# Hash attention and a mixture of adapters on one core: a bank begun by a copy, block turns and loads moved, products of the second last pair moved

## The chip, the cores and the metric

The kernel runs on one core of a Trainium2 chip. TensorE (PE) multiplies, VectorE (DVE), ScalarE (ACT) and GpSimd (POOL) work element by element, SyncE (SP) issues transfers that 16 DMA engines carry out. The metric is the device time of one execution in microseconds; lower is better. The median over several runs counts.

## What is computed

There are 4 batches of 8 heads, 768 positions and 64 features. Each position of q and k gets a bucket from the signs of six projections; a query sees only keys of its own bucket. Rows whose mask is empty fall back to a mean over all keys, which is why the kernel adds a very small uniform term.

```python
q_bits = (einsum('bhsd,dk->bhsk', q, proj) > 0)      # k the same
mask = q_bucket[:, :, :, None] == k_bucket[:, :, None, :]
scores = where(mask, q @ k.T / sqrt(D), -1e9)
attn = exp(scores - max); attn = attn / (sum(attn) + 1e-9)
x = (attn @ v) as (B*S, H*D)
logits = x @ w_gate                                   # two best of eight experts
delta = sum over the two experts e of w_e * ((x @ A[e]) @ B[e])
out = x + delta
```

## The kernel before, in words

The 32 heads are worked off as 16 pairs (p = 0 to 15, two heads h of one batch each, four pairs to a batch), and each pair in six slots (s = 0 to 5). The order of every engine's queue is written out by hand: `slot` (L698) first emits the scores of the slot, then the list that `work` (L710) has put together for it. All queues run strictly in order, so an instruction that waits holds up all that stand behind it on its engine.

In each slot TensorE makes scores for 1536 columns (`score`, four matmuls of L283) in one of two groups of PSUM banks, and ScalarE exponentiates them into P (L286). Per slot there is room for other work on TensorE: the products of P and v (`pvk`, L303, six per block of keys and per head), the hash of a later pair (`hash`, L193), transposes of q (`trq`, L241), the logits of the adapters (`lgz`, L407) and the products that give delta (`delta`, L506 and L527).

The sum for a head is gathered in one PSUM bank (pool ps_v, one buffer). `uni` (L288) begins that bank: a matmul with a matrix of 2^-56 against the column sum of v, repeated six times, writes 390 columns. `pvk` then adds to it, and `norm` (L321 and L323) divides by the gathered sum on VectorE and frees the bank. Head 1 of pair p-1 is begun in slot 0 of pair p and ended in slot 1; head 0 of pair p is begun in slot 3 or 4 and ended in slot 5.

Other work runs ahead: `loadqk` (L152) loads q of pair p+4 in slot 2 and k of pair p+4 in slot 3 (slot 4 in pairs that have logits), `loadv` (L160) loads v of pair p+2 in slot 2. `turn32` (L180, VectorE) turns 32x32 blocks of q and k into R, four turns per pair, in slots 0 to 3 (`turns`): the last half of k of pair p+2, both halves of q of pair p+3 and the first half of k of pair p+3. `hash` (slot 2) reads R of pair p+2, `sign` (L205) compares, `signs_out` and `signs_in` (L212, L220) carry the signs through DRAM into the operands of the scores (aug). `natcast` (L232) casts q and k on GpSimd, `turnk` (L253) transposes k by DMA, `shift` (L261) moves half of it on GpSimd. `vcast` (L168 to L173) casts v on GpSimd and then forms its column sum in three additions. `to_bf` (L333) and `turn` (L339) prepare x for the logits.

The adapters of batch b are done while batch b+1 is attended to: `plan` (L870) gives each pair which three rows I of logits it makes, in which slot, and which deltas (a dictionary from slot to row). Odd pairs from 5 on have logits in slot 3 (`route1`, `gates`, `gsum`: L416 to L455; the weights' exponential L428 stands on ScalarE ahead of the scores' exponential of slot 4), and from 7 on one delta in slot 0; even pairs from 6 on have two deltas in slots 3 and 4. Logits, hashes, transposes and deltas all use one bank (pool ps_m, one buffer). The last two pairs have an order of their own.

Of the kernel before, what the change touches and what calls it, by code (L numbers as in the profile page):

```python
# [12 lines left out]
F32 = mybir.dt.float32  # L13
# [6 lines left out]
class Emitter:  # L20
# [142 lines left out]
    def vcast(self, p):  # L163
        if p >= self.N:
            return
        nc, T, D = self.nc, self.T, self.D
        vn, vb = self.vn[p], self.vb[p % 3]
        nc.gpsimd.tensor_copy(out=vb[:, :, 0:T, 0:D], in_=vn)  # L168
        s3 = self.smallp.tile([self.P, 2, 3, D], F32, tag="vs3", name=f"vs3_{p}")
        nc.gpsimd.tensor_add(out=s3, in0=vn[:, :, 0:3, :], in1=vn[:, :, 3:6, :])  # L170
        s1 = self.smallp.tile([self.P, 2, D], F32, tag="vs1", name=f"vs1_{p}")
        nc.gpsimd.tensor_add(out=s1, in0=s3[:, :, 0, :], in1=s3[:, :, 1, :])
        nc.gpsimd.tensor_add(out=vb[:, :, T, 0:D], in0=s1, in1=s3[:, :, 2, :])  # L173
# [111 lines left out]
            at += w  # L285
        nc.scalar.activation(out=self.P_[p][:, s * W:end], in_=ps, func=ACT.Exp, scale=128.0)  # L286

    def uni(self, p, h):  # L288
        T, D = self.T, self.D
        pv = self.pv[p, h] = self.vt([self.P, T, D + 1], F32, f"pv{p}_{h}")  # L290
        self.nc.tensor.matmul(out=pv, lhsT=self.eps,  # L291
                              rhs=self.vb[p % 3][:, h, T:T + 1, :].to_broadcast([self.P, T, D + 1]),
                              start=True, stop=False, skip_group_check=True)

    def pvk(self, p, h, kts):
        if p < 0:
# [352 lines left out]
    def first(self, s):  # L649
        if s == 0:  # L650
            self.hash1(1, self.h1)
            self.turn32(1, 0, 0)
            self.turn32(1, 1, 0)
            self.sign1(self.h1, (0, 1))
            self.natcast(1, 0)
            self.natcast(1, 1)
            self.loadv(1)
            self.loadqk(3, 0)
        if s == 1:
            self.hash(1, (0,))  # L660
# [4 lines left out]
            self.vcast(0)  # L665
        if s == 2:
            self.trq(1, 0)
            self.qcopy(1)
            self.shift(1, 0)
        if s == 3:  # L670
            self.trq(1, 1)
            self.qcopy(1, 1)
            self.turn32(1, 0, 1)
            self.turn32(1, 1, 1)
            self.shift(1, 1)
            self.signs_in(1, (0,))
            self.loadqk(4, 0)
            self.natcast(2, 0)
            self.natcast(2, 1)
            self.turn32(2, 0, 0)  # L680
            self.turn32(2, 0, 1)
        if s == 4:
            self.hash(1, (1,))
            self.sign(1, (1,))
            self.signs_out(1, (1,))
            self.loadqk(4, 1)
            self.turn32(2, 1, 0)
            self.signs_in(1, (1,))
            self.vcast(1)
        if s == 5:  # L690
            self.trq(2)
            self.qcopy(2)
            self.turn32(2, 1, 1)
            self.shift(2, 0)
# [15 lines left out]
    def work(self, p):  # L710
        N = self.N
        W = [[] for _ in range(6)]
        add = lambda s, *f: W[s].append(f)
        b, L, Ls, D = self.plan(p)
        n1, n2, n3, n4 = (p + i for i in range(1, 5))
        last = p == N - 1
        new = p == N - 2

        if last:
            pv = {0: [(p - 1, 1, (2, 3))], 1: [(p - 1, 1, (4, 5))]}  # L720
        elif new:
            pv = {0: [(p - 1, 1, (0, 1, 2))], 1: [(p - 1, 1, (3,))], 2: [(p - 1, 1, (4, 5))]}
        elif p:
            d = int(p == 1)
            pv = {d: [(p - 1, 1, (0, 1, 2))], d + 1: [(p - 1, 1, (3, 4, 5))]}
        else:
            pv = {}
        if p == 0:
            pv.update({3: [(p, 0, (0, 1, 2))], 5: [(p, 0, (3, 4, 5))]})
        elif new:  # L730
            pv.update({3: [(p, 0, (0, 1, 2))], 4: [(p, 0, (3, 4, 5))], 5: [(p, 1, (0, 1))]})
        elif p == 1 or L:
            pv.update({4: [(p, 0, (0, 1, 2, 3))], 5: [(p, 0, (4, 5))]})
        elif not last:
            pv.update({3: [(p, 0, (0, 1))], 4: [(p, 0, (2, 3))], 5: [(p, 0, (4, 5))]})

        def values(s):
            for g, h, kts in pv.get(s, ()):
                if kts[0] == 0 and g == p:
                    add(s, "uni", g, h)  # L740
                add(s, "pvk", g, h, kts)
                if kts[-1] == 5:
                    add(s, "norm", g, h)

        if p == 0:
            for s in range(6):
                add(s, "first", s)
                values(s)
        elif p == 1:
            self.second(add, values)  # L750
        else:

            if not last:
                add(0, "uni", p - 1, 1)
            values(0)
            if 0 in D and not last:
                add(0, "delta", *D[0])
            add(0, "turns", p, 0)
            add(0, "shift", n1, 1)
            add(0, "signs_in", n1)  # L760
            add(0, "natcast", n2, 1)

            values(1)
            if last:
                add(1, "to_bf", p - 1)
                add(1, "turn", p - 1)
            add(1, "turns", p, 1)

            values(2)
            add(2, "loadqk", n4, 0)  # L770
            add(2, "loadv", n2)
            add(2, "hash", n2)
            add(2, "turns", p, 2)
            add(2, "shift", n2, 0)
            if last:
                add(2, "lasts", 2)
            else:
                add(2, "to_bf", p - 1)

            add(3, "sign", n2)  # L780
            add(3, "signs_out", n2)
# [12 lines left out]
            if p < 5:  # L794
                add(4, "trq", n2, 1)
                add(4, "qcopy", n2, 1)
            if L:
                for f in ("gates", "zt_dma", "gsum"):
                    add(Ls + 1, f, b, L)
                add(4, "loadqk", n4, 1)  # L800
            values(5)
            add(5, "trq", n3)
            add(5, "qcopy", n3)

        if L:
            for i in L:
                add(Ls, "lgz", b, L, i)
            add(Ls, "route1", b, L)
        for s in sorted(D):
            d, i = D[s]  # L810
            if s or last:
                add(s, "delta", d, i)
            if p < N - 2 and i in (2, 3):
                add(s, "store", d, 1, i % 2)
            elif i % 2:
                add(s, "store", d, i // 2)
        if last:
            for s in range(3, 6):
                add(s, "lasts", s)
        for i, at in enumerate(((1, 5), (2, 4), (2, 5), (3, 4), (3, 5), (4, 4))):  # L820
            if at[0] == p:
                add(at[1], "load_moe", i)
        for i, at in enumerate(((4, 5), (5, 4))):
            if at[0] == p:
                add(at[1], "cast_moe", i)
        return W

    def second(self, add, values):
# [27 lines left out]
        add(3, "turns", 1, 3)  # L856
        add(3, "natcast", 4, 0)
        add(3, "vcast", 2)
        values(4)
# [163 lines left out]
```

## Time and profile before

| what | value |
|---|---|
| three runs | 161.24, 162.39, 164.31 us (median 162.39) |
| the profiled execution | 162.86 us, of which the span from first to last instruction is 161.1 us |
| TensorE busy | 148.5 us (92%) |
| ScalarE busy | 143.0 us (89%) |
| GpSimd busy | 111.6 us (69%) |
| VectorE busy | 108.9 us (68%) |
| transfers | 33.04 MB, mean 205 GB/s |

Most rows below name engine, line, what is written and what is read, how often, and the busy time. A row of the timeline starts with the time in us from the span's start; what stands in brackets at its end is the idle time before it and what ended it. A table by stretches gives for each stretch its length, then the busy time of each engine, the granted TensorE clock, the share of the DMA engines and GB/s. Its stretches here run from the first exponential of one pair to that of the next (pair 6 begins at 61.96 us, pair 9 at 87.12, pair 14 at 131.76).

### The profile page before, as it was taken

The numbers are of one execution on the slowest core, as the hardware profiler recorded it, in microseconds if no ns is written. First come the engines' busy times: TensorE is split into PE (matmuls) and PEld (weight loads), VectorE is DVE, ScalarE is ACT, GpSimd is POOL, SyncE is SP. The second block draws the span as 40 slices with busy tenths as digits, with TensorE's granted clock in tenths as the row PEclk, the third lists the DMA queues.
The fourth block names the chain that finished last, engine by engine and source line by source line (L and its number), as shares of the span: only waits on it lengthen the run. The fifth ranks groups of instructions, "written<-read, shape, count | busy, mean of one in ns | idle before, by whom it ended". The sixth has DMA issues, their size and how long they took to land.

```text
span 161.1 us, 5327 instructions
## 1 busy us (share of the span) xinstructions
PE 148.5 (92%) x2169; PEld 101.0 (63%) x2170; DVE 108.9 (68%) x292; ACT 143.0 (89%) x125; POOL 111.6 (69%) x166
## 2 busy tenths in 40 slices
PE   6988999999999999999999979999979999999830
PEld 3335676676767667676766656667756666689510
DVE  5698985746464976778686676686656545665880
ACT  3688899999999999999999969998997999899640
POOL 7783999998969795969397955979399742620060
PEclk9999999999999999999999999999999999999995
DMA  4994469899998895989979996999978750665055
GB/s 149 320 371 131 133 194 192 225 233 215 214 215 195 241 206 146 247 167 373 198 208 233 291 259 164 225 215 361 233 158 197 232 82 16 119 267 180 6 201 192
DMA packets 57595, 33.04 MB, mean 205 GB/s; under 512 B 42978, under 2 KB 55266, under 8 KB 57570
## 3 DMA queue, kind: packets, MB, share of 16 engines
q1 hardware_dynamic: 57296, 32.43, 79.8%
q8 instruction: 17, 0.28, 0.7%
q10 hardware_dynamic: 274, 0.27, 0.5%
q14 instruction: 8, 0.07, 0.1%
HBM read 20.16 MB, written 7.03 MB: 169 GB/s over the span
## 4 chain that ended last, share of the span: by engine, by line
PE 67%; DVE 11%; DMA 10%; POOL 5%; issue 2%; ACT 1%; DVEq 0%; SPq 0%; POOLq 0%
PE s L283 28%; PE pv L303 16%; DMA nat<-in_k_dram 6%; PE hs L193 6%; DMA aug<-nb 3%; PE tr L241 3%; PE pv L291 3%; PE dl L506 2%; DVE R L180 2%; PE lz L407 2%; PE warm L647 2%; POOL nb L232 1%; DVE aug L571 1%; DVE x L323 1%; DVE aug L590 1%
## 5 line engine op out<-in xcount | busy, mean ns | idle before, releaser
L286 ACT ACTIVATE P<-s 128x1536 bf16<-128x1536 f32 x96 | 133.2, 1454 | 4.0 <-PE s L283 2.7
L283 PE MATMUL s<-aug 71*128 71x512 bf16 (+2 forms) x432 | 78.5, 308 | 0.9 <-DVE aug L571 0.7
L283 PEld LDWEIGHTS <-aug 71*128 71x128 bf16 x432 | 34.6, 97 | 21.4 <-issue 5.5
L303 PEld LDWEIGHTS <-P 128*128 128x128 bf16 x1080 | 42.1, 98 | 8.2
L303 PE MATMUL pv<-vb,P 128*128 128x65 bf16 x1080 | 44.3, 193 | 0.0
L261 POOL COPY aug<-aug 64x768 bf16<-64x768 bf16 x30 | 24.8, 827 | 17.6 <-DMA aug<-nb 13.8
L180 DVE STREAM_TRANSPOSE R<-nat 128x384 f32<-128x384 f32 x62 | 33.2, 559 | 5.6 <-DMA nat<-in_k_dram 4.6
L232 POOL CAST nb<-nat 128x768 bf16<-128x768 f32 x30 | 24.6, 823 | 1.0
L333 POOL CAST xb<-x 128x768 bf16<-128x768 f32 x15 | 12.3, 822 | 11.7 <-DVE x L323 4.8
L527 DVE SCALAR_TENSOR_TENSOR acc<-dl,rt,x 128x512 f32<-128x512 f32 x18 | 13.5, 748 | 7.9 <-PE dl L506 7.9
L323 DVE TENSOR_TENSOR x<-pv,ri 128x384 f32<-128x384 f32 x30 | 16.7, 558 | 1.0
L170 POOL TENSOR_TENSOR vs<-vn 128x384 f32<-128x384 f32 x16 | 15.9, 994 | 0.0
L321 DVE RECIPROCAL ri<-pv 128x6 f32<-128x6 f32 x30 | 5.8, 193 | 14.2 <-PE pv L303 14.2
L247 DVE TENSOR_SCALAR aug<-tr 128x768 bf16<-128x768 bf16 x20 | 11.0, 550 | 5.7 <-PE tr L241 2.3
L193 PE MATMUL hs<-R,hst 128*32 128x192 f32 x240 | 14.0, 332 | 0.0
L168 POOL CAST vb<-vn 128x768 bf16<-128x768 f32 x16 | 13.2, 826 | 0.3 <-DMA vn<-in_v_dram 0.3
L241 PE MATMUL tr<-ident_bf,nb 128*128 128x128 bf16 x120 | 10.0, 219 | 0.9 <-DVE ss L453 0.9
L193 PEld LDWEIGHTS hs<-R,hst 128*32 128x32 f32 x240 | 6.7, 109 | 6.3 <-DVE ri L321 3.8
L291 PE MATMUL pv<-vb,eps 128*128 128x390 bf16 x30 | 10.1, 336 | 0.6 <-DVE gw L436 0.3
L525 POOL TENSOR_TENSOR acc<-acc,x 128x512 f32<-128x512 f32 x2 | 2.5, 1266 | 9.2 <-ACT acc L524 9.1
L241 PEld LDWEIGHTS <-nb 128*128 128x128 bf16 x120 | 7.3, 97 | 1.9 <-POOL vb L173 1.0
L173 POOL TENSOR_TENSOR vb<-vs,vs 128x128 bf16<-128x128 f32 x16 | 7.3, 457 | 1.3
(111 smaller groups left out, 112.1 us busy)
## 6 DMA issues: line engine op xcount, KB each, us to landing
vn<-in_v_dram SPq DMA_DIRECT2D x16, 384.0 KB, 7.1
nat<-in_q_dram SPq DMA_DIRECT2D x15, 384.0 KB
nat<-in_k_dram SPq DMA_DIRECT2D x15, 384.0 KB, 3.5
out_dram<-acc SPq DMA_DIRECT2D x7, 512.0 KB, 3.9
out_dram<-acc SPq DMA_DIRECT2D x9, 256.0 KB, 5.6
dr<-sg SPq DMA_DIRECT2D x14, 48.0 KB, 2.9
aug<-dr SPq DMA_DIRECT2D x14, 48.0 KB
nat<-in_q_dram SPq DMA_DIRECT2D x2, 192.0 KB
```

Source lines behind the costliest of these rows:

```text
L170: nc.gpsimd.tensor_add(out=s3, in0=vn[:, :, 0:3, :], in1=vn[:, :, 3:6, :])
L180: self.nc.vector.transpose(out=self.R[p][:, i, h, :], in_=self.nat[p][:, i, h, :])
L193: nc.tensor.matmul(out=hs[32 * j:32 * j + 32], lhsT=self.hst[:, hf].rearrange("p b i -> p (b i)"), rhs=rhs, start=(hf == 0), stop=(hf == 1 ...
L232: self.nc.gpsimd.tensor_copy(out=self.nb[p][:, i].rearrange("p t h d -> p h t d"), in_=self.nat[p][:, i].rearrange("p h (t d) -> p h t d", ...
L241: self.nc.tensor.transpose(out=tr[:, t, :], in_=self.nb[p][:, i, t].rearrange("p h d -> p (h d)"), identity=self.ident_bf)
L261: self.nc.gpsimd.tensor_copy(out=a[0:64, :, 2 + i, :], in_=a[64:128, :, i, :])
L283: nc.tensor.matmul(out=ps[:, o:o + w].rearrange("p (t c) -> p t c", c=P), lhsT=aug[0:71, kt, 2 * h + 1, :], rhs=rhs, start=True, stop=True)
L286: nc.scalar.activation(out=self.P_[p][:, s * W:end], in_=ps, func=ACT.Exp, scale=128.0)
L291: self.nc.tensor.matmul(out=pv, lhsT=self.eps, rhs=self.vb[p % 3][:, h, T:T + 1, :].to_broadcast([self.P, T, D + 1]), start=True, stop=Fal ...
L303: self.nc.tensor.matmul(out=pv[:, i, :], lhsT=self.P_[p][:, o:o + P], rhs=vb[:, h, kt, :], start=False, stop=(kt == T - 1), skip_group_che ...
L323: nc.vector.tensor_tensor(out=self.x[b][:, :, c:c + D], in0=pv[:, :, 0:D], in1=ri.unsqueeze(2).to_broadcast([P, T, D]), op=ALU.mult)
L527: nc.vector.scalar_tensor_tensor(out=out, in0=ps, scalar=rt, in1=self.x[b][:, i, :], op0=ALU.mult, op1=ALU.add)
```

## The change

- `uni` for head 1 of pair p-1 now takes a whole bank (512 columns) and, for p from 3 to 13 (`seeded`), first makes one more matmul, of 65 columns, that puts the column sum of v of pair p into columns 390 to 454. The `uni` of head 0 of pair p is left out for these eleven pairs. In its place, right after `norm` of head 1 of pair p-1 in slot 1, VectorE copies the 65 columns six times over columns 0 to 389 (`seed`), and the products of head 0 are added to that.
- `vsum` is split from `vcast`: the sum of v of pair p+1 is formed at the start of pair p (before: the sum followed the cast at the end of the pair). `loadv` loads v of pair p+3 behind the k load (before: of pair p+2 behind the q load); pair 2 loads v of pairs 4 and 5.
- `turns` gives other halves to other slots: odd pairs turn both halves of k of pair p+2 in slot 0 and the first half of q of pair p+3 in slot 2; even pairs turn three halves of pair p+2 in slot 0 and the two halves of q of pair p+3 in slots 2 and 3 (or 4).
- `sign` follows `hash` directly in slot 2, ahead of that slot's turn.
- Pair 14: its logits move from slot 1 to slot 2, its deltas from slots 3, 4, 5 to slots 1 and 4, and one delta goes to pair 15, which has four (slots 0 to 3). `turn` moves from slot 3 to slot 4. Three blocks of products that stood in slots 1 and 2 stand in slot 1.

```diff
     def vcast(self, p):
...
+        self.nc.gpsimd.tensor_copy(out=self.vb[p % 3][:, :, 0:T, 0:D], in_=self.vn[p])
+
+    def vsum(self, p):
...
-        nc.gpsimd.tensor_copy(out=vb[:, :, 0:T, 0:D], in_=vn)
...
-    def uni(self, p, h):
+    def uni(self, p, h, nxt=None):
         T, D = self.T, self.D
-        pv = self.pv[p, h] = self.vt([self.P, T, D + 1], F32, f"pv{p}_{h}")
+        n = T * (D + 1)
+        V = self.V = self.vt([self.P, 512], F32, f"pv{p}_{h}")
+        pv = self.pv[p, h] = V[:, 0:n].rearrange("p (t d) -> p t d", t=T)
+        if nxt is not None and self.seeded(nxt):
+            self.nc.tensor.matmul(out=V[:, n:n + D + 1], lhsT=self.eps, rhs=self.vb[nxt % 3][:, 0, T, :],
+                                  start=True, stop=True)
         self.nc.tensor.matmul(out=pv, lhsT=self.eps,
...
+    def seeded(self, p):
+        return 2 < p < self.N - 2
+
+    def seed(self, p):
...
+        pv = self.pv[p, 0] = self.V[:, 0:n].rearrange("p (t d) -> p t d", t=T)
+        self.nc.vector.tensor_copy(out=pv, in_=self.V[:, n:n + D + 1].unsqueeze(1).to_broadcast([self.P, T, D + 1]))
...
         elif new:
-            pv = {0: [(p - 1, 1, (0, 1, 2))], 1: [(p - 1, 1, (3,))], 2: [(p - 1, 1, (4, 5))]}
+            pv = {0: [(p - 1, 1, (0, 1, 2))], 1: [(p - 1, 1, (5,))]}
...
-                if kts[0] == 0 and g == p:
+                if kts[0] == 0 and g == p and (h or not self.seeded(p)):
                     add(s, "uni", g, h)
                 add(s, "pvk", g, h, kts)
                 if kts[-1] == 5:
                     add(s, "norm", g, h)
+                    if g < p and self.seeded(p):
+                        add(s, "seed", p)
...
+            add(0, "turns", p, 0)
             if not last:
-                add(0, "uni", p - 1, 1)
+                add(0, "uni", p - 1, 1, p)
             values(0)
             if 0 in D and not last:
                 add(0, "delta", *D[0])
-            add(0, "turns", p, 0)
+            add(0, "turns", p, 1)
+            if p > 2:
+                add(0, "vsum", n1)
             add(0, "shift", n1, 1)
             add(0, "signs_in", n1)
+            if p == 2:
+                add(0, "loadv", 4)
             add(0, "natcast", n2, 1)
 
+            if new:
+                add(1, "pvk", p - 1, 1, (3, 4))
+                add(1, "delta", *D[1])
             values(1)
...
-            add(1, "turns", p, 1)
 
             values(2)
             add(2, "loadqk", n4, 0)
-            add(2, "loadv", n2)
             add(2, "hash", n2)
+            add(2, "sign", n2)
             add(2, "turns", p, 2)
             add(2, "shift", n2, 0)
+            if p == 2:
+                add(2, "vsum", n1)
...
-            add(3, "sign", n2)
             add(3, "signs_out", n2)
             if p > 4:
                 add(3, "turnk", n2)
             values(3)
-            add(3, "turns", p, 3)
             if not last and p % 2 == 0:
-                add(3, "turn", p - 1)
+                add(3 + new, "turn", p - 1)
             if not L:
                 add(3, "loadqk", n4, 1)
+                add(3, "loadv", n3)
...
                 add(4, "loadqk", n4, 1)
+                add(4, "loadv", n3)
+            add(4, "turns", p, 4)
...
-            if s or last:
+            if last or s > 1:
                 add(s, "delta", d, i)
+            if s == 3 and not last:
+                add(s, "turns", p, 3)
...
     def turns(self, p, s):
-        c = {1: {0: (0, 2), 1: (1, 3), 3: (4, 5)}, 2: {0: (2, 3), 1: (4,), 2: (5,), 3: (6,)}}.get(
-            p, {0: (3,), 1: (4,), 2: (5,), 3: (6,)})
+        c = {1: {0: (0, 2), 1: (1, 3), 3: (4, 5)}, 2: {1: (2, 3), 2: (4,), 4: (5,)}, 4: {1: (1, 2, 3), 2: (4,), 4: (5,)}}.get(
+            p, {0: (2,), 1: (3,), 2: (4,)} if p % 2 else {1: (1, 2, 3), 2: (4,), 3: (5,)})
...
         if p == N - 2:
-            return b, G1, 1, {3: (b, 0), 4: (b, 1), 5: (b, 2)}
+            return b, G1, 2, {1: (b, 0), 4: (b, 1)}
         if p == N - 1:
-            return b, None, 0, {0: (b, 3), 1: (b, 4), 2: (b, 5)}
+            return b, None, 0, {i - 2: (b, i) for i in range(2, 6)}
```

In `turns` the number n stands for pair p+2 (n under 4) or p+3, tensor q (n mod 4 under 2) or k, and the half n mod 2. The entry under 0 is issued at the start of slot 0, the one under 1 at the end of slot 0's products and delta, and those under 2, 3 and 4 in these slots.

More of the change, by code (lines that the diff above doesn't have):

```diff
@@ L165, in vcast @@
             return
+        T, D = self.T, self.D
+        self.nc.gpsimd.tensor_copy(out=self.vb[p % 3][:, :, 0:T, 0:D], in_=self.vn[p])
+    def vsum(self, p):
+        if p >= self.N:
+            return
         nc, T, D = self.nc, self.T, self.D
         vn, vb = self.vn[p], self.vb[p % 3]
-        nc.gpsimd.tensor_copy(out=vb[:, :, 0:T, 0:D], in_=vn)
         s3 = self.smallp.tile([self.P, 2, 3, D], F32, tag="vs3", name=f"vs3_{p}")
@@ L665, in first @@
             self.vcast(0)
+            self.vsum(0)
         if s == 2:
@@ L689, in first @@
             self.vcast(1)
+            self.vsum(1)
         if s == 5:
@@ L858, in second @@
         add(3, "vcast", 2)
+        add(3, "vsum", 2)
         values(4)
```

2 lines of the change are left out of this document (added).

## The prediction

> **What bounds the kernel now.** I read the busy shares first, then a table by stretches of one pair each, then the waits, then ScalarE's and VectorE's timelines where the table shows a bad pair.
>
> ```profile
> PE 148.5 (92%) x2169; PEld 101.0 (63%) x2170; DVE 108.9 (68%) x292; ACT 143.0 (89%) x125; POOL 111.6 (69%) x166
> ```
>
> TensorE and ScalarE are both near full, so an average can't name the bound. The stretches can.
>
> ```profile
> 45.37:53.46 8.09, 8.09 (x130) 5.66 (x129) 4.75 (x12) 8.09 (x7) 6.70 (x9) 1.00 0.85 177
> 53.46:61.96 8.50, 8.50 (x134) 5.98 (x133) 7.40 (x23) 8.48 (x8) 6.05 (x8) 1.00 1.04 211
> 61.96:70.17 8.21, 8.21 (x125) 5.54 (x124) 5.71 (x13) 8.21 (x8) 6.71 (x9) 1.00 0.94 203
> 70.17:78.91 8.74, 8.74 (x135) 6.10 (x134) 6.75 (x21) 8.55 (x9) 6.71 (x9) 1.00 1.06 281
> 78.91:87.12 8.21, 8.21 (x125) 5.54 (x124) 5.72 (x13) 8.21 (x8) 6.70 (x9) 1.00 0.87 206
> 87.12:97.01 9.89, 9.02 (x141) 6.42 (x140) 6.86 (x22) 8.44 (x8) 6.72 (x10) 1.00 1.11 260
> 97.01:105.03 8.02, 8.02 (x123) 5.36 (x120) 5.43 (x12) 8.02 (x8) 6.41 (x9) 1.00 0.84 203
> 105.03:114.19 9.16, 9.12 (x145) 6.54 (x144) 6.87 (x22) 8.47 (x9) 7.00 (x10) 1.00 1.07 287
> 114.19:123.15 8.96, 8.10 (x118) 5.34 (x115) 5.27 (x12) 8.23 (x7) 7.17 (x10) 1.00 0.89 201
> 123.15:131.76 8.61, 8.38 (x128) 5.77 (x127) 4.99 (x17) 8.44 (x8) 5.94 (x9) 1.00 0.68 170
> 131.76:141.04 9.28, 8.94 (x143) 6.55 (x142) 5.14 (x16) 8.67 (x8) 3.82 (x6) 1.00 0.32 65
> ```
>
> These are pairs 4 to 14: length, then busy PE, PEld, DVE, ACT, POOL. Pair 7 (with logits) takes 8.74 and pair 8 (without) 8.21, and TensorE is busy for all of both. Pairs 9 to 12 have the same work as 7 and 8 in turn and take 9.89, 8.02, 9.16 and 8.96; in 9 and 12 TensorE stands idle for 0.9 us. ScalarE's timeline shows why, and its floor:
>
> ```profile
> 94.22 0.22 ACT L428 ACTIVATE e<-d 128x24 f32<-128x24 f32 x1 [1.33 <-DVE d L418]
> ...
> 111.40 0.22 ACT L428 ACTIVATE e<-d 128x24 f32<-128x24 f32 x1 [0.61 <-DVE d L418]
> 111.53 9.48 ACT L286 ACTIVATE P<-s 128x1536 bf16<-128x1536 f32 x7
> ```
>
> Seven exponentials that ran on end took 9.48 us. One lasts 1.45 (the page's mean, 1454 ns), and they overlap a little, so they start (9.48 - 1.45) / 6 = 1.34 us apart: six, a pair, need 8.03 us. No pair can be shorter. The small exponential of the adapters stands ahead of slot 4's and waited for VectorE (d). VectorE in turn waited:
>
> ```profile
> POOL aug L261 <- DMA aug<-nb: 13.8, 8, 3.4
> ...
> DVE R L180 <- DMA nat<-in_k_dram: 4.6, 3, 1.9
> ```
>
> ```profile
> 93.19 0.58 DVE L180 STREAM_TRANSPOSE R<-nat 128x384 f32<-128x384 f32 x1 [1.91 <-DMA nat<-in_k_dram]
> ...
> 110.36 0.58 DVE L180 STREAM_TRANSPOSE R<-nat 128x384 f32<-128x384 f32 x1 [1.18 <-DMA nat<-in_k_dram]
> ...
> 119.41 0.58 DVE L180 STREAM_TRANSPOSE R<-nat 128x384 f32<-128x384 f32 x1 [1.55 <-DMA nat<-in_k_dram]
> ```
>
> All three waits are the turn of the first half of k of pair p+3, in slot 3 of pairs 9, 11 and 12. The logits' maximum (9, 11) and a delta's end (12) stand behind it. So three things bound these stages: TensorE in pairs 5 to 8 and 13, ScalarE in pair 4 and those like it (8.09 against 8.03), late k loads in 9, 11 and 12.
>
> **The change part by part.**
>
> *Turns.* The turn that waited (n = 6) is gone from slot 3. A first half of k loaded in slot 3 or 4 of pair p is now turned in slot 0 of pair p+2 instead of slot 3 of pair p+1: three slots later, 3 x 1.34 = 4.0 us by the spacing above, twice the longest wait of 1.91. What goes is the excess of pairs 9 to 12 over two undisturbed pairs of each kind: 9.89 + 8.02 + 9.16 + 8.96 = 36.03, less 2 x (8.74 + 8.21) = 33.90: **2.13 us**. What is late next is TensorE itself, which is full in pairs 7 and 8. The turns of q keep some six slots from load to turn. The bound below: the waits return elsewhere, 0 gained; the bound above: all three idle times, 4.64.
>
> *The bank.* For eleven pairs TensorE drops a matmul of 390 columns and gains one of 65.
>
> ```profile
> 69.94 0.34 PE L291 MATMUL pv<-vb,eps 128*128 128x390 bf16 x1
> 70.12 0.71 PE L303 MATMUL pv<-vb,P 128*128 128x65 bf16 x18
> ...
> 75.91 0.90 PE L303 MATMUL pv<-vb,P 128*128 128x65 bf16 x24
> ```
>
> ```profile
> 131.63 0.34 PE L291 MATMUL pv<-vb,eps 128*128 128x390 bf16 x1 [0.23 <-DVE x L323]
> ...
> 136.06 0.33 PE L291 MATMUL pv<-vb,eps 128*128 128x390 bf16 x1 [0.32 <-DVE gw L436]
> ...
> 136.78 0.38 PE L506 MATMUL dl<-Bcat,zT 128*128 128x512 bf16 x1
> 136.99 0.81 PE L283 MATMUL s<-aug 71*128 71x512 bf16 x4
> ...
> 149.25 0.22 PE L349 MATMUL pvJ<-vb,eps 128*128 128x65 bf16 x2
> 149.31 0.52 PE L407 MATMUL lzI<-wa,xT 128*128 128x136 bf16 x6
> ```
>
> From start to start the wide one takes 0.18 (69.94 to 70.12), two of 65 columns take 0.06 (149.25 to 149.31), so one 0.03: 0.15 saved per pair. It counts where TensorE is the bound: pairs 5 to 13, nine times 0.15 = **1.35 us**; pair 8's 8.21 - 0.15 = 8.06 still lies above ScalarE's 8.03. In pairs 3 and 4 ScalarE sets the time, and I take 0 (0.05 each at most).
>
> ```profile
> L180 DVE STREAM_TRANSPOSE R<-nat 128x384 f32<-128x384 f32 x62 | 33.2, 559 | 5.6 <-DMA nat<-in_k_dram 4.6 <-DMA nat<-in_q_dram 0.9
> L323 DVE TENSOR_TENSOR x<-pv,ri 128x384 f32<-128x384 f32 x30 | 16.7, 558 | 1.0
> L170 POOL TENSOR_TENSOR vs<-vn 128x384 f32<-128x384 f32 x16 | 15.9, 994 | 0.0
> ```
>
> ```profile
> 72.52 0.56 DVE L323 TENSOR_TENSOR x<-pv,ri 128x384 f32<-128x384 f32 x1
> ```
>
> VectorE gains eleven copies of 390 numbers from PSUM. No row shows a copy within PSUM; the nearest, L323, also reads PSUM and takes 0.56 for 384. I take 0.56 (0.4 to 0.8): 6.2 us of VectorE in all. In pair 7 the copy follows the division that ends at 73.08 and is over at 73.64; the products that need it start at 75.91, so 2.3 us cover it. In even pairs they stand a slot earlier, which leaves about 1 us. Odd pairs lose one turn of 0.56 (three instead of four) and even pairs gain one: VectorE then holds 6.75 + 0.56 - 0.56 = 6.8 us of about 8.6, and 5.72 + 1.12 = 6.8 of 8.06. Cost 0; with the cover gone, up to 0.56 x 11 = 6.2. The 65-column matmul waits for nothing that the wide matmul behind it doesn't wait for; its sum is formed nearly a pair ahead.
>
> *Sums, loads, signs.* GpSimd's order stays what it was but for one thing: from pair 3 on the sum that stood at a pair's end is that of the next pair. That puts one more set of three additions (0.99 the largest, L170) into pairs 2 and 3, under 3 us, and pairs like 4, where GpSimd works 6.70 of 8.09, take that up. Cost 0 (0 to 1.0, if a transpose of q in pair 2 or 3 waits for its cast). One v load more falls into pair 2; no one waits for v. `sign` ahead of a turn leaves 0.56 earlier, and with it signs and the k transposes, which stand next on SP now that the v load is behind k. That shortens GpSimd's wait of 13.8 us, which today delays nothing that ends last: 0. SP also gets v between k and the signs' read (see the third rival).
>
> *Pairs 14 and 15.* Pair 14 loses one delta product (0.21, from 136.78 to 136.99) and the wait of 0.32 ahead of the bank's start, because its division no longer stands behind the route's steps on VectorE; the wait of 0.23 at 131.63 stays. Pair 15 gains the product, ahead of other work in slot 3. I take 0.32 + 0.21 - 0.21 = **0.3 us**. The bounds: pair 14's whole excess, 9.28 - 8.03 = 1.25, gained, or two products (0.42) lost in pair 15. `turn` of pair 14, one slot later, is wanted only at pair 15's end. Nothing else behind 149.3 changes.
>
> *Sum.* 2.13 + 1.35 + 0.3 = 3.8 us off the profiled execution, whose time is 162.86: 159.1. The median of the runs is 162.39, 0.47 lower, which would give 158.6. Whether that 0.47 is in the late loads, which go, or elsewhere, the page doesn't say; I take the middle, **158.9**.
>
> **The rivals.**
>
> *1. The waits for transfers move, they don't go.* The DMA share is 1.07 to 1.11 in pairs 9 and 11, and the change moves no fewer bytes. If the next consumer (GpSimd's 13.8 us wait, or a cast) now ends last, only the bank and the end gain: 162.4 - 1.35 - 0.3 = 160.7. For it: crowded odd pairs. Against: GpSimd works only 6.41 us of pair 10, more idle time than in pair 8, and that pair is the shortest of all with 8.02.
>
> *2. The bank's start gains nothing*, because the copy or the deltas' common bank hold TensorE as long as the matmul did, or ScalarE becomes the bound in all even pairs: 162.4 - 2.13 - 0.3 = 160.0. Against: TensorE is full to the last in pairs 7 and 8, and the copy has 1 to 2.3 us of cover.
>
> *3. Slower: signs come late.* The v load (384 KB) now stands between k and the signs' read on SP.
>
> ```profile
> 88.85 0.29 SPq L220 DMA_DIRECT2D aug<-dr  x1
> ...
> 90.23 0.90 SPq L160 DMA_DIRECT2D vn<-in_v_dram  x1
> ```
>
> ```profile
> 95.98 0.81 PE L283 MATMUL s<-aug 71*128 71x512 bf16 x4
> ```
>
> ```profile
> dr<-sg SPq DMA_DIRECT2D x14, 48.0 KB, 2.9
> ```
>
> ```profile
> 105.74 4.59 DMA nat<-in_k_dram
> ...
> 114.12 5.26 DMA nat<-in_k_dram
> ```
>
> The read is issued at 88.85 and needed by pair 10's first scores at 95.98: 7.1 us, and 1.15 less when pair 9 is no longer stretched (9.89 to 8.74): 6.0. No view shows when it lands. The nearest rows are the signs' write, of the same size, 2.9 us after issue, and the late k loads, 4.6 to 5.3. The v load adds its 0.9 of issue and, as my estimate, as much again for its bytes: 4.7 to 7.1. So it is close. It decides from a landing 6.0 us after the old issue time on. A wait of 1 us ahead of each of pairs 8, 10, 12 and 14 eats the whole gain; 2 us in each gives 158.9 + 8 = 167, the middle of the two 165. For it: the Trainium skill, DMA: Bandwidth & Descriptors, section Queues, rings and completion order, says that each DMA engine takes descriptors in ring order, so that v's bytes go ahead of the signs; no view of this run shows the order on one ring. Against: the signs are also written earlier, since the v load no longer stands ahead of `signs_out`, and the median of 2.9 holds for more reads than the three worst k loads do.
>
> **How the numbers follow.** The forecast with its parts: 0.66, by itself 157.6 to 160.2 (the turns from 1.7 to 2.6, the bank 0.9 to 1.5, the end 0 to 0.9). Rival 1: 0.15, rival 2: 0.11, rival 3: 0.08. Two per cent of 162.39 is 3.25 us, so under 159.1 counts as faster (2% is about what a measurement of this kernel can tell from no change): somewhat over two thirds of the forecast's range by weight, 0.46. Within two per cent: the rest of the forecast, 0.20, rivals 1 and 2, 0.26, and 0.03 of rival 3: 0.49. Slower by more than 2%, over 165.6: 0.05. The range is 157.3 to 161.6: it takes in rivals 1 and 2 and leaves out rival 3 and the tails.
>
> **What would show it.** VectorE's wait for k loads drops from 4.6 to under 1; no idle time over 0.3 ahead of L428 in pairs 9 and 11; pairs 9 and 11 at 8.6, 6, 8, 10 and 12 at 8.05 to 8.15, pair 7 at 8.6; 19 wide starts of the bank and 11 narrow ones, eleven copies near 0.56 with no PE wait behind them; pair 15's first exponential about 0.5 sooner after pair 14's than 9.28. I am wrong if TensorE shows idle time ahead of a pair's first scores (signs), or GpSimd's casts hold up transposes in slot 5, or pairs 9 to 12 still differ from 7 and 8.

## The result and the profile after

The changed kernel takes 160.49 us (median of 20 runs, 158.90 to 163.19), the kernel before 162.52 us in runs beside them (20, 160.91 to 164.89). The ratio is 0.987, with a 95% interval of 0.984 to 0.990: 2.0 us or 1.3% faster, inside the range that was forecast and about 1.6 us short of its middle. (Medians are over all runs, while a ratio leaves out the runs more than 1.5% above the fastest of their kernel.) The profiled execution has a span of 159.5 us and a time of 161.24, 0.75 above the median, so it holds somewhat more idle time than most.

The page's busy time of each engine:

```profile
PE 147.3 (92%) x2168; PEld 100.6 (63%) x2170; DVE 116.2 (73%) x303; ACT 143.0 (90%) x125; POOL 112.0 (70%) x166
```

VectorE has 7.3 us more than before (116.2 against 108.9), 6.3 of it in the copies; TensorE has 1.2 less. The windows by pair, 6 to 14, with the columns as before (length; PE, PEld, DVE, ACT, POOL; clock, DMA share, GB/s):

```profile
61.80:70.24 8.44, 8.37 (x128) 5.70 (x129) 7.23 (x16) 8.20 (x7) 6.35 (x9) 1.00 1.00 209
70.24:78.66 8.42, 8.42 (x134) 5.96 (x132) 6.60 (x21) 8.38 (x8) 6.76 (x9) 1.00 1.25 283
78.66:88.10 9.44, 8.38 (x126) 5.66 (x124) 7.60 (x16) 8.41 (x7) 6.26 (x8) 1.00 0.88 171
88.10:96.69 8.59, 8.59 (x136) 6.12 (x135) 6.15 (x19) 8.44 (x7) 6.92 (x10) 1.00 1.12 296
96.69:105.23 8.54, 8.14 (x125) 5.55 (x124) 7.28 (x16) 8.23 (x6) 6.19 (x9) 1.00 1.07 205
105.23:113.70 8.47, 8.47 (x134) 6.01 (x133) 6.17 (x20) 8.36 (x7) 7.04 (x10) 1.00 1.07 306
113.70:121.87 8.17, 8.17 (x128) 5.56 (x126) 6.96 (x15) 8.17 (x7) 6.45 (x10) 1.00 0.92 196
121.87:130.25 8.38, 8.18 (x127) 5.63 (x125) 6.02 (x19) 8.34 (x9) 7.55 (x11) 1.00 0.77 203
130.25:138.88 8.63, 8.55 (x141) 6.46 (x141) 4.91 (x15) 8.63 (x9) 1.60 (x2) 1.00 0.14 28
```

Pairs 9 to 12 now take 8.59, 8.54, 8.47 and 8.17, together 2.3 us less than before. But pair 8, undisturbed before (8.21), now takes 9.44: 1.2 of the gain went there, and 0.2 to pair 6 (8.21 before, now 8.44). Two groups of VectorE, then the waits:

```profile
L185 DVE STREAM_TRANSPOSE R<-nat 128x384 f32<-128x384 f32 x62 | 33.1, 559 | 0.5 <-DMA nat<-in_q_dram 0.4
L313 DVE COPY pv<-pv 128x390 f32<-128x390 f32 x11 | 6.3, 572 | 0.4
```

```profile
POOL aug L266 <- DMA aug<-nb: 8.7, 6, 3.2
POOL vs L175 <- DMA vn<-in_v_dram: 2.7, 4, 0.9
PE s L288 <- DMA aug<-dr: 1.2, 2, 0.8
```

The turns wait no more for k (4.6 us before; what is left is 0.4 for q). The eleven copies take 0.57 each, and no row of TensorE waits for one; the matmul of 65 columns takes 0.04 from start to start (78.46 to 78.50), where 0.03 was reckoned. GpSimd's wait for transposes fell from 13.8 to 8.7, and it now waits a little for v (vs). New is the last row: TensorE's scores wait for the signs' read (aug<-dr). The two longest waits of TensorE in the pairs, and the one at the end of pair 2:

```profile
36.06 0.51 PE L246 MATMUL tr<-ident_bf,nb 128*128 128x128 bf16 x6 [0.20 <-POOL nb L237]
...
87.19 0.81 PE L288 MATMUL s<-aug 71*128 71x512 bf16 x4 [0.82 <-DMA aug<-dr]
...
104.32 0.81 PE L288 MATMUL s<-aug 71*128 71x512 bf16 x4 [0.40 <-DMA aug<-dr]
```

The first is the end of pair 2 (8.47 long, 8.14 before), the others are the first scores of pairs 9 and 11, waited for at the end of pairs 8 and 10 (in pair 8 TensorE waited another 0.24 for the transposed zT). So part of what the k loads had cost came back as a wait for signs. Why the signs were late stands in SP's timeline (start, time that the issue takes, line):

```profile
72.26 0.35 SPq L556 DMA_DIRECT2D out_dram<-acc  x1
72.66 1.13 SPq L152 DMA_DIRECT2D nat<-in_q_dram  x1
74.22 1.02 SPq L217 DMA_DIRECT2D dr<-sg  x1
75.34 3.30 SPq L258 DMA_TRANSPOSE aug<-nb  x1
78.74 1.38 SPq L512 DMA_TRANSPOSE zT<-zm  x1
80.17 0.57 SPq L152 DMA_DIRECT2D nat<-in_k_dram  x1
80.80 1.82 SPq L160 DMA_DIRECT2D vn<-in_v_dram  x1
82.79 0.30 SPq L225 DMA_DIRECT2D aug<-dr  x1
```

Here the issue of a transfer occupies SP: the transpose holds it for 3.30 us, the v load for 1.82, and the signs' read leaves only at 82.79, 4.1 us into pair 8. The chain of what ended last then has its flight:

```profile
82.79 4.27 DMA aug<-dr
```

### The profile page after: what moved, and what is told of

Read it like the earlier page. It is cut to its first block, busy times and chain, and to the rows that moved or that the text cites. A ratio compares the mean times of both kernels' runs of the same rounds, so it can differ in the third digit from the quotient of the medians.

```text
span 159.5 us, 5350 instructions
## 1 busy us (share of the span) xinstructions
PE 147.3 (92%) x2168; PEld 100.6 (63%) x2170; DVE 116.2 (73%) x303; ACT 143.0 (90%) x125; POOL 112.0 (70%) x166
## 2 busy tenths in 40 slices
DMA packets 57595, 33.04 MB, mean 207 GB/s; under 512 B 42978, under 2 KB 55266, under 8 KB 57570
## 3 DMA queue, kind: packets, MB, share of 16 engines
HBM read 20.16 MB, written 7.03 MB: 170 GB/s over the span
## 4 chain that ended last, share of the span: by engine, by line
PE 53%; POOL 14%; DVE 12%; DMA 8%; ACT 4%; issue 3%; SPq 2%; POOLq 0%
PE s L288 22%; PE pv L323 12%; DMA aug<-dr 5%; POOL aug L266 4%; POOL nb L237 4%; ACT P L291 3%; PE hs L198 3%; DMA aug<-nb 3%; PE dl L526 2%; DVE R L185 2%; DVE acc L547 2%; PE lz L427 2%; POOL vs L175 2%; PE tr L246 2%; PE warm L667 2%
## 5 line engine op out<-in xcount | busy, mean ns | idle before, releaser
L210 DVE TENSOR_SCALAR sg<-hs,ssc 128x192 bf16<-128x192 f32 (+1 forms) x16 | 6.7, 418 | 2.6 <-PE hs L198 1.7
L177 POOL TENSOR_TENSOR vs<-vs 128x128 f32<-128x128 f32 x16 | 7.3, 455 | 1.3
```

## The experiments

The kernels ran in three groups of four, each beside the kernel before: the first two groups on one chip (kernel before: 163.12 and 163.36 us), the third on another (163.23). Each reading of waits or pairs is that of one profiled execution. Where lengths of pairs are given, they run from first exponential to first exponential in ScalarE's timeline. The theory to begin with: the moved turns and the copy give what was forecast, and late signs take part of it back because v stands ahead of them. The first rival: transfers are so full in pairs 7 to 12 that somebody waits whatever the order.

**The changed kernel again** (no edit).

> The changed kernel once more, beside the variants. Over its 20 runs it was 2.0 us faster than before (162.5 to 160.5). Theory (late signs): the turns' gain is partly given back because the v load stands ahead of the signs' read, so this should again be 1.5 to 2.5 us under before, with an idle PE ahead of the first scores of some pairs (wait for aug<-dr, about 1 us in all). Rival (chance): the wait for aug<-dr of 1.2 us belongs to the one profiled execution and is absent here.

Measured: 160.64 us, ratio 0.987 (0.981 to 0.992). The stall was in pair 7 this time (9.82), pair 8 took 8.10. It was again the signs' read, in the chain:

```profile
71.80 6.67 DMA aug<-dr
```

In these two executions of one kernel the place of the longest stall differs and its kind is the same.

**The signs' read ahead of the v load**, which stands behind it in slot 0 of the next pair.

```diff
-            if p == 2:
-                add(0, "loadv", 4)
+            add(0, "loadv", n2)
...
-                add(3, "loadv", n3)
...
-                add(4, "loadv", n3)
```

> As the changed kernel, but the v load stands behind the signs' read (slot 0 of the next pair) instead of ahead of it. Theory (late signs): no PE wait for aug<-dr, and 1.0 to 1.6 us faster than the changed kernel, so 3.0 to 3.6 under before. Rival (chance, or the transfers are simply full): within 0.4 us of the changed kernel, the wait either stays or moves to GpSimd's sums, which now get v half a pair later.

Measured: 163.75 us, with five of six runs from 162.9 to 164.9 and one of 159.5, too uneven for a ratio, and no gain is shown. Of the profiled execution (163.46 us) two waits and a row of TensorE:

```profile
POOL vs L175 <- DMA vn<-in_v_dram: 11.0, 7, 3.1
...
PE s L288 <- DMA aug<-dr: 0.3, 1, 0.3
```

```profile
122.80 0.51 PE L246 MATMUL tr<-ident_bf,nb 128*128 128x128 bf16 x6 [1.34 <-POOL nb L237]
```

In this execution the signs, now ahead, were nearly in time and v was late. (The Trainium skill, DMA: Bandwidth & Descriptors, section Queues, rings and completion order, has each DMA engine take descriptors in ring order; the wait for signs, down from 1.2 to 0.3 us, agrees, though it follows as well from the read's earlier issue.) In pair 12 GpSimd's sum of v waited 2.85 us and the copy behind it 2.13 for a transpose (aug<-nb); its cast (nb) stood behind both, and TensorE's transposes waited for that. "No one waits for v" in the prediction holds only where v is loaded as early as in the kernel before, whose page has 0.3 us of such waits.

**The change without the copied bank.**

```diff
-        return 2 < p < self.N - 2
+        return False
```

> As the changed kernel, but no bank is begun by VectorE: all 30 banks are begun by the wide matmul. My sum priced the copy at 0.15 us in nine TensorE-bound pairs: 1.35 us slower than the changed kernel, and pairs 7, 9 and 11 at 8.6 instead of 8.45. Rival: the copy gains nothing (the division and the common bank hold TensorE as long), under 0.4 us of difference.

Measured: 162.12 us, ratio 0.990 (0.985 to 0.995), against 0.987 with it: by times the copy can't be told from nothing. By pairs without a stall it can. Without it pairs 5, 9, 11 and 13 take 8.41, 8.67, 8.62 and 8.56; with it, in an execution without stalls (the changed kernel without stores, below), 8.31, 8.52, 8.43 and 8.38: 0.10 to 0.19 less each. (The stores aren't the reason: with them, the version with mended ends below has 8.31, 8.42, 8.47 and 8.40.) In pairs 6 and 8 it is 0.09 and -0.02. My estimate for nine pairs, five odd ones at 0.15 and four even ones at 0.04, is 0.9 us.

**The change with the turns where they were.**

```diff
...
-            add(0, "turns", p, 1)
...
+            add(1, "turns", p, 1)
...
+            add(3, "turns", p, 3)
...
-            add(4, "turns", p, 4)
...
-        c = {..., {0: (2,), 1: (3,), 2: (4,)} if p % 2 else {1: (1, 2, 3), 2: (4,), 3: (5,)})
+        c = {..., {0: (3,), 1: (4,), 2: (5,), 3: (6,)})
```

> As the changed kernel, but the block turns stand where they stood before (k's first half in slot 3 of the pair after its load). My sum priced the move at 2.13 us: 1.5 to 2.5 us slower than the changed kernel, with VectorE waiting for k loads (4.6 us before, 0 after) and gaps ahead of the adapters' exponential. Rival (chance): the k waits were those of one execution or came from the old place of the v load, under 0.5 us of difference.

Measured: 163.56 us, ratio 1.002 (0.997 to 1.006). Without the moved turns nothing is gained, and the wait is back:

```profile
DVE R L185 <- DMA nat<-in_k_dram: 3.9, 4, 1.5
```

From 0.987 to 1.002 is 1.5%, about 2.4 us.

**The moved turns alone, in the kernel before** (the edit of the change, nothing else).

```diff
...
+            add(0, "turns", p, 1)
...
-            add(1, "turns", p, 1)
...
-        c = {..., {0: (3,), 1: (4,), 2: (5,), 3: (6,)})
+        c = {..., {0: (2,), 1: (3,), 2: (4,)} if p % 2 else {1: (1, 2, 3), 2: (4,), 3: (5,)})
```

> The kernel before with the new places of the block turns and nothing else. Theory (my sum): 2.1 us under before, no VectorE wait for k loads, pairs 9 to 12 like pairs 7 and 8. Rival (the turns' gain needs the new place of the v load or the earlier sign): under 1 us.

Measured: 161.62 us, ratio 0.988 (0.981 to 0.996). No turn waits for k any more, but pair 12 took 9.97. GpSimd stood still 4.54 us for a transpose (aug<-nb), which landed 7.66 us after its issue; its casts stood behind that, and TensorE's transposes waited for a cast:

```profile
117.01 0.82 POOL L261 COPY aug<-aug 64x768 bf16<-64x768 bf16 x1 [4.54 <-DMA aug<-nb]
```

```profile
121.31 0.51 PE L241 MATMUL tr<-ident_bf,nb 128*128 128x128 bf16 x6 [1.34 <-POOL nb L232]
```

So the turns by themselves bring 1.2% (0.4 to 1.9), nearly all that was measured, and in a kernel that has v where it always was, a stall of the same size appears elsewhere. The order of v and signs alone does not explain it.

**The v load behind q, two slots earlier.**

```diff
             add(2, "loadqk", n4, 0)
+            add(2, "loadv", n3)
...
-                add(3, "loadv", n3)
...
-                add(4, "loadv", n3)
```

> As the changed kernel, but the v load of pair p+3 stands in slot 2 behind the q load, where a v load stood before the change, so neither ahead of the signs' read nor behind it. Theory (crowded transfers: what stands between a k load and the signs' read makes the signs late, and a v load that lands late holds GpSimd's sums): neither wait, 0.8 to 1.5 us under the changed kernel, about 3 under before. Rival (the transfers are full, whatever is put first, something else is late): within 0.4 us of the changed kernel, with the wait on zT, aug<-nb or nat instead.

Measured: 162.15 us, ratio 0.992 (0.988 to 0.996): no better than the change. Nothing waits for signs or v any more, but GpSimd's aug waits 12.7 us for transposes, and in pair 10 (10.16) TensorE waits behind it:

```profile
POOL aug L266 <- DMA aug<-nb: 12.7, 6, 4.8
```

```profile
103.67 0.51 PE L246 MATMUL tr<-ident_bf,nb 128*128 128x128 bf16 x6 [1.30 <-POOL nb L237]
```

The other pairs are nearly undisturbed (pair 11 takes 8.60). With this my theory that the place of v is the cause fell, and the rival that transfers are full was left: its kind of wait came, though not its time, within 0.4 us of the change.

**The ends mended**: the first copied bank is pair 4's, pair 2's sum goes back to its end, one product goes from pair 15 back to pair 14.

```diff
-        return 2 < p < self.N - 2
+        return 3 < p < self.N - 2
...
-            if p == 2:
-                add(2, "vsum", n1)
...
+            if p == 2:
+                add(3, "vsum", n1)
...
-            return b, G1, 2, {1: (b, 0), 4: (b, 1)}
+            return b, G1, 2, {1: (b, 0), 4: (b, 1), 5: (b, 2)}
...
-            return b, None, 0, {i - 2: (b, i) for i in range(2, 6)}
+            return b, None, 0, {0: (b, 3), 1: (b, 4), 2: (b, 5)}
```

> As the changed kernel, but the first pair with a copied bank is 4, so that the sum for pair 3 stands at the end of pair 2 as before, and the delta that went from pair 14 to pair 15 is back in pair 14's slot 5. Theory: pair 2 ends in 8.1 instead of 8.5 (its last cast no longer stands behind the sum) and pair 15 takes 8.4 instead of 8.9 while pair 14 takes at most 8.9: 0.6 to 0.9 us under the changed kernel. Rival: the loss comes back in pairs 3 and 15's end, within 0.3 us.

Measured: 160.39 us, ratio 0.985 (0.980 to 0.990). By times this is the change's own; by pairs, pair 2 is back from 8.47 to 8.13, and pairs 14 and 15 take 8.95 + 8.38 = 17.33 against 8.63 + 8.94 = 17.57 in the change and 17.66 before. Pair 10 still stalls (9.14); TensorE waits 0.43 us there for zT and 0.33 for signs.

**Both, ends mended and v behind q**; against the ends mended:

```diff
+            add(2, "loadv", n3)
...
-                add(3, "loadv", n3)
...
-                add(4, "loadv", n3)
```

> Both mendings at once: the v load behind q, and the two ends. Theory: 1.5 to 2.3 us under the changed kernel, 3.5 to 4.3 under before (ratio 0.974 to 0.978). Rival (transfers are full): the ends' 0.6 to 0.9 alone.

Measured: 162.04 us, ratio 0.985 (0.980 to 0.991), with runs from 159.6 to 164.9. Pair 9 took 9.72, where TensorE waited 1.03 us for the transposed x (xT). The theory fell here too: another order of the same bytes doesn't end the stalls.

**No stores**: the change and the kernel before, both without the stores that run while pairs are still loaded. The expectations call them those of batches 0 to 2. In fact they are those of batches 0 and 1, so half of the output isn't written (the page has 3.88 MB written to HBM instead of 7.03).

```diff
-            if p < N - 2 and i in (2, 3):
-                add(s, "store", d, 1, i % 2)
+            if p < N - 2:
+                pass
             elif i % 2:
```

> The changed kernel without the stores of batches 0 to 2 of the output (they are left out, so most of the output is never written; all else is computed). Theory (the stalls of 1 to 2 us in pairs 7 to 12 come from transfers that are nearly full there, and the stores are the part of them that nothing waits for): pairs 7 to 12 all lie between 8.1 and 8.7, no wait of a sum, a transpose or a product for a DMA over 0.5 us, and the median is 1.0 to 2.0 us below the changed kernel's 160.5: 158.5 to 159.5. Rival (the late landings are the order of the queue alone: signs behind v): the late signs' read stays, with one pair over 9.3, and the median stays within 0.5 of 160.5.

> The kernel before without the stores of batches 0 to 2 of the output (left out, as in the other run). Theory (transfers full): the waits of the block turns for the loads of k (4.6 us before) fall below 1 us and the kernel comes to 159.5 to 160.8, so that the change is worth only the copied bank's 1.0 and 0 to 0.4 beside it between the two kernels without stores. Rival (the turns are too close to their loads with or without stores): the waits for k stay at 3 us or more and the difference between the two kernels without stores is 2.0 or more.

Measured: 158.76 us for the change (6 runs, 158.2 to 158.9; ratio to the kernel before with its stores 0.974, 0.969 to 0.979) and 160.53 for the other (159.7 to 161.4; 0.986, 0.981 to 0.992). Pairs 8 to 10 of the change, then 9 to 11 of the kernel before, both without stores:

```profile
78.63:86.79 8.16, 8.16 (x127) 5.56 (x126) 6.95 (x15) 8.16 (x7) 6.12 (x9) 1.00 1.00 213
86.79:95.31 8.52, 8.52 (x137) 6.12 (x135) 7.22 (x21) 8.47 (x9) 6.74 (x9) 1.00 1.02 202
95.31:103.40 8.09, 8.09 (x127) 5.50 (x126) 6.86 (x15) 8.09 (x6) 6.39 (x9) 1.00 0.99 208
```

```profile
86.52:95.25 8.73, 8.73 (x135) 6.09 (x134) 6.75 (x21) 8.54 (x8) 7.11 (x10) 1.00 0.85 199
95.25:103.46 8.21, 8.21 (x125) 5.54 (x124) 5.74 (x13) 8.21 (x7) 6.07 (x9) 1.00 1.02 202
103.46:112.20 8.74, 8.74 (x135) 6.10 (x134) 6.83 (x21) 8.55 (x9) 6.70 (x9) 1.00 0.95 209
```

TensorE is busy for the whole of each: no stall is left in either, and the turns of the kernel before no longer wait for k at all. The rival that the turns stand too close to their loads, stores or not, falls for this execution. SP's timeline of the change without stores, for the same stretch as above:

```profile
71.65 0.37 SPq L152 DMA_DIRECT2D nat<-in_q_dram  x1
74.18 0.37 SPq L217 DMA_DIRECT2D dr<-sg  x1
74.64 1.39 SPq L258 DMA_TRANSPOSE aug<-nb  x1
77.17 1.18 SPq L512 DMA_TRANSPOSE zT<-zm  x1
78.41 0.58 SPq L152 DMA_DIRECT2D nat<-in_k_dram  x1
79.03 0.47 SPq L160 DMA_DIRECT2D vn<-in_v_dram  x1
79.68 0.29 SPq L225 DMA_DIRECT2D aug<-dr  x1
```

The same transpose holds SP for 1.39 us instead of 3.30, the v load for 0.47 instead of 1.82, and the signs' read leaves at 79.68, 3.1 us sooner at the same place in the work (pair 8 starts at 78.63 and 78.66). Three things did not come as expected. GpSimd's sums of v still waited 0.8 to 1.15 us in pairs 8, 10 and 11 of the change, over the 0.5 of the theory, though TensorE is busy all the same. The change also had one wait for signs where no store could be the reason, ahead of pair 4 (0.70 us). There the issue of the signs' read held SP for 3.10 us, right behind two loads of adapter weights:

```profile
37.76 1.10 SPq L123 DMA_DIRECT2D w<-in_moe_A_dram  x2
39.31 3.10 SPq L225 DMA_DIRECT2D aug<-dr  x1
```

So it need not be a store that SP stands behind. That the stalls in pairs 6 to 12 go with the stores is shown; whether the stores as such count there, or only the 3.15 MB less to move (29.89 instead of 33.04), no run tells apart. And the difference of the two medians is 1.8 us, between the 1.4 at most of the theory and the rival's 2.0. The two profiled executions, which agree with each other in pairs 5 to 13 but for the change, differ there by 76.1 - 74.6 = 1.5 us; the profiled execution of the kernel before is the fastest of its six, and where the others lost up to 1.8 us more isn't recorded here.

**The copy made twice** (each copy of `seed` issued two times).

```diff
+        for _ in range(2):
             self.nc.vector.tensor_copy(out=pv, ...)
```

> The changed kernel with each of VectorE's eleven copies into a bank made twice (same result, 11 x 0.58 = 6.4 us more of VectorE). Theory (the copy lies in cover): within 0.5 us of the changed kernel. Rival (nothing covers it; TensorE's sums of the first head wait for it): 3 to 6 us slower, and the sums of v with the first head wait for VectorE in each pair.

Measured: 161.92 us, ratio 0.994 (0.989 to 0.999) against 0.987: some 1.1 us more. Neither: most of 6.3 us is covered, not all. Rows of VectorE and of TensorE in pair 7 (a line number above 313 is one higher here):

```profile
73.48 1.18 DVE L314 COPY pv<-pv 128x390 f32<-128x390 f32 x2
74.57 0.41 DVE L210 TENSOR_SCALAR sg<-hs,ssc 128x192 bf16<-128x192 f32 x1
```

```profile
75.03 0.87 PE L428 MATMUL lz<-wa,xT 128*128 128x136 bf16 x12 [0.21 <-DVE sg L210]
```

The first to notice isn't the product that adds to the bank but the logits, which wait until the signs behind the copy have been taken out of PSUM. Slot 3 of the odd pairs grows from 1.46 to 1.78 us, so of the 0.6 that the second copy adds (1.18 for two) only about 0.3 was covered. In even pairs it is covered (pair 8: 8.12).

**The best version: ends mended, batch 1's stores later.** With the ends mended SP issued batch 1's stores as four, two in pair 11 and two in pair 13 (the expectation counts three). Here they are three, two in pair 13 and one in pair 14.

```diff
+            if d == 1:
+                pass
-            if p < N - 2 and i in (2, 3):
+            elif p < N - 2 and i in (2, 3):
...
+        if p == N - 3:
+            add(2, "store", 1, 0)
+            add(4, "store", 1, 1)
+        if new:
+            add(0, "store", 1, 2)
```

> The version with the mended ends (first copied bank in pair 4, the sum of v of pair 2 at its end, one product of pair 15 back in pair 14), and batch 1's three stores, which stand in pairs 10 to 13, moved to pairs 13 and 14. Theory (the stalls come from full transfers): the stall of pair 10 goes and nothing as long comes in pairs 13 and 14, where the loads of q and k have ended: 0.5 to 1.0 us below the version with mended ends (160.4), ratio to the kernel before 0.979 to 0.983. Rival (a stall comes back in another pair, or the acc buffers held longer make a product wait): 0.985 or more, with a pair over 9.0.

Measured: 158.94 us (6 runs, 158.1 to 159.2), ratio 0.975 (0.970 to 0.981): faster than both kernels, with the whole output written, and better than the 0.979 to 0.983 of the theory. Pairs 9 to 12:

```profile
86.44:94.86 8.42, 8.42 (x134) 5.96 (x132) 6.97 (x21) 8.38 (x8) 7.82 (x12) 1.00 1.11 308
94.86:103.10 8.24, 8.21 (x126) 5.61 (x124) 7.03 (x16) 8.24 (x7) 6.03 (x9) 1.00 1.01 203
103.10:111.58 8.48, 8.48 (x134) 6.01 (x133) 6.53 (x21) 8.37 (x9) 6.99 (x10) 1.00 1.09 236
111.58:119.74 8.16, 8.16 (x127) 5.56 (x126) 6.95 (x16) 8.16 (x8) 7.62 (x11) 1.00 0.72 170
```

No pair stalls (pair 7, at 8.60, is 0.2 longer than elsewhere); 13 and 14, which now have the stores, take 8.38 and 8.96. How it gets there is only partly shown. Its stretch of pairs is 0.8 us shorter than with mended ends, but the stall of pair 10 that is gone (9.14 to 8.24) lies ahead of the first store that was moved, so this one execution can't credit the edit with it. Another 0.56 is behind the last exponential, 11.10 us against 11.64 to 11.67 in the executions that write every store in its old place, and 11.18 in those without stores. It arises behind the issue of the last store, which comes 7.23 us after the last exponential both here and with mended ends. I have no cause for it that the traces bear out.

## Why the prediction was right, and where not

The forecast was 158.9 within 157.3 to 161.6, and the measured 160.49 lies between it and its first rival (160.7), 1.6 us from the one and 0.2 from the other. By itself the forecast with its parts went only to 160.2: the time lies in the range because the range took in the rivals. And two signs that the prediction named for being wrong came, idle time of TensorE ahead of a pair's first scores (pairs 9 and 11), and transposes held up by a cast in slot 5 (pair 2). Step by step:

*Turns, 2.13 us.* The mechanism was right. The three waits for k are gone, no small exponential waits ahead of slot 4 in pairs 9 and 11, and pairs 9 to 12 lost 2.3 us. Undone, they cost 2.4 us; done alone, they bring 1.2%, about 1.9. What failed is the sentence "what is late next is TensorE itself". Next were the signs' read in the change, transposes (aug<-nb) in the turns alone and with v behind q, v with the signs first, and xT with both mendings. The waits moved in part (rival 1), and the form they took in the changed kernel was that of rival 3, though only twice, ahead of pairs 9 and 11, and not ahead of every even pair: 0.82 and 0.40 of waiting, 1.2 us more in pair 8. Rival 3 counted a landing 6.0 us after issue as the limit and took the issue as fixed, but for 0.9 of the v load's own. In fact the issue itself came 3.1 us later than in the execution without stores: among the issues ahead of it, the transpose held SP 1.91 us longer and the v load 1.35. Stores, which neither the forecast nor a rival named, are what TensorE's waits in the middle went with.

*The bank, 1.35 us.* Right in odd pairs (0.15 measured, 0.15 forecast) and too much in even ones, which gained 0.04 each: 0.9 in all. The step reckoned by pair, but ScalarE's floor holds by slot: in no execution do two exponentials start closer than 1.33 us (six make 7.98, where the prediction had 8.03). In even pairs the matmul that went stood in slot 3, which takes 1.41 us without the copy and 1.35 with it: the floor leaves 0.06 of the 0.15. In odd pairs from 7 on it stood in slot 4, 1.46 us without and 1.33 with the copy, so nearly all of it shows. Rival 2, nothing gained at the bank's start, falls for the odd pairs. The copy's own 0.57 was sized right, its cover was not. "2.3 us cover it" looked only at who reads the bank. `sign` on VectorE stands behind it too, and the logits behind that: the one copy and about 0.3 us more are covered in odd pairs. It cost nothing, but narrowly.

*Not counted: the turns' new places.* Where neither kernel stalls, pairs 5 to 13 are 1.5 us shorter with the change. The copy is 0.9 of that; the other 0.6 has to come from the rest of the change in the same pairs. With the turns alone, odd pairs are already some 0.08 shorter (8.65 against 8.74 in pair 7, where slot 3 goes from 1.50 to 1.46 and slot 4 from 1.51 to 1.46); where the remainder comes from stays open.

*Sums of v, "0 (0 to 1.0)".* The bound that was named came true at a third: pair 2 is 0.33 longer, since a transpose waits for a cast behind one more set of sums. Moving that sum back removed it.

*Pairs 14 and 15, 0.3 us.* Measured 17.66 - 17.57 = 0.1. Pair 14 gained more than was forecast (9.28 to 8.63), pair 15 lost 0.55 (8.39 to 8.94): the product put into its slot 3 stands ahead of the last pair's own sums (slot 3 takes 1.99 us instead of 1.44). The step counted the product's 0.21 on both sides and not that place.

*The sum.* The forecast's figure is near that of an execution without stalls: 158.8 with no stores, 158.9 with later ones and mended ends (both also have some 0.5 us less behind the last exponential). What separates it from 160.5 is 0.33 in pair 2, 0.2 at the end and, by subtraction, about 1 us of stalls in the middle. That the bank's 0.45 too much and the 0.6 not counted nearly cancel is luck. That the stalls in the middle vanish without stores is shown; which store delays which transfer, whether any other bytes taken away would do the same, and why pair 10's went in the last version, stays open.

## What to carry to other kernels

Before crediting a removed wait in full, find what the late transfer is late behind, and ask which consumer is the next to meet it: here k, q, v, signs and transposes all ran on one queue, and nearly every new order had a new victim. Look at how long each issue holds the queue's engine, not only at landings. Transfers that nobody waits for, such as stores, are the first to move out of a stretch whose DMA share is near 1. (The Trainium skill, Perfetto Trace Analysis, section DMA Optimizations, proposes an issuing engine of its own for outputs; no run here tried that.) And when an operation is added to an engine, its cover ends at the first thing queued behind it that someone needs, not at its own reader.

## What the runs showed of the hardware that was not expected

- The time that the issue of a DMA takes on SP isn't fixed. The same kind of transpose (aug<-nb) held SP for 1.39 us in the execution without stores and for 3.30 at the same place with them; a v load for 0.47 and 1.82. In the execution without stores a read of signs held it for 0.29 us in pair 8 and for 3.10 behind two loads of weights, ahead of pair 4.
- A small read (48 KB of signs) took 4.27 and 6.67 us from issue to landing, the first behind a load of k and one of v, the second behind both and a store.
- The spread of a kernel's times went with its stores: 158.9 to 163.2 us for the changed kernel in twenty runs and 159.9 to 166.9 in six more, 158.2 to 158.9 in six without them, 158.1 to 159.2 in six with those of batch 1 later and the ends mended.
- VectorE copied 390 numbers per partition from one part of a PSUM bank to another, out of 65 read six times over, in 0.57 us: the time of a division of 384 (0.56).
